# Weight tiles moved by 16 and 32 bytes relative to the moving operands, in a windowed attention, gated FFN and channel MLP kernel

## Chip, cores, metric

One NeuronCore of a Trainium2 chip runs the program. The metric is the time of one execution in microseconds on the device; below, the median of several runs.

## What is computed

Attention over 4 batches, 8 heads, 576 positions and 64 dimensions a head, with a window of 32 (plain for heads 0 to 3, each fourth position for heads 4 to 7); then a gated feed-forward layer with a time shift; then a channel MLP on top of a rank-32 mix over positions:

```python
attn = softmax(where(mask, q @ k.T / 8, -1e9)) @ v          # x: (4, 576, 512)
xk = mu_k * x + (1 - mu_k) * x_prev;  xr = mu_r * x + (1 - mu_r) * x_prev
x = sigmoid(xr @ w_r) * (relu(xk @ w_k) ** 2 @ w_v)         # 512 -> 1024 -> 512
u = x + (x.T @ U @ V).T
out = u + relu(u @ w_ch1) @ w_ch2                           # 512 -> 2048 -> 512
```

## The kernel before

The products run on TensorE as fp32r, each value split into a high and a low part, so that a product takes three matmuls: high weights by high data, low weights by high data, high weights by low data. The low part is what is left after the high part was rounded off (`hi_lo` in the first layers, `part_split` in the last).

The work stands in three blocks in time, read from the timeline.

- **Up to 60 us**: attention of the first batch, loading and converting the weights of the gated layer, and that layer on the first 288 positions in plain fp32 (L1110, L1125).
- **60 to about 340 us**: the gated layer on the other seven pieces of 288 positions. Its three matmuls are L1097, L1098 and L1099, each 128x128 weights by 288 columns. The moving data are the tiles `xk` (in box A's place) and `k2s` (in box B's), 16 pieces of 288 columns each. Between them lie the attention of the later batches (L958, L996, L1014), and the rank-32 mix (L1223 transposes, L1241, L1258).
- **About 340 us to the end**: the channel MLP. It runs in nine visits (`VISITS`) over five groups of positions, each over four or eight of the eight tiles j of 256 hidden channels. Its first product is L1374 to L1376, its second L1462 to L1464, all 128x128 weights by 256 columns. Seven products of sums of blocks stand for the eight of a two-by-two block product; VectorE and ScalarE form the sums.

**Where the tiles lie.** A tile pool gives each tag its place in SBUF once; a tile is made when the first operation on it is recorded, and a new tag goes behind those already there. The weights are pieces of 512 words, 2,048 bytes, in a pool of 42 under the tag `w` (`piece`, names `wh`, `wl`, and `wx` for the plain fp32 ones). In the last block the weights of each fourth tile j (j % 4 == 3) lie in box A and box B instead, into which `take` puts them with `part`; by then `xk` and `k2s` are done. `SHIFT` moves what is in such a box by some words: by 16 words in A, and in B by 16 for units below 10 (weights) and by 64 for those from 10 on (hidden values, which are moving operands). A word is 4 bytes.

`Lazy.__call__` puts a small tile, a pad, ahead of the first tile of the tags in `PADS`: 16 words ahead of `w`, 48 words ahead of `pt`, which lies behind the pool `w`.

By the addresses in the built program all tiles of pool `w` start at 224 (mod 256). The moving tiles (boxes `raw`, `w64`, `x`, `sig`, `xk`, `k2s`, hidden values in B) start at 160; of the pieces of 288 columns (1,152 bytes) the odd ones start at 32. The weights in boxes A and B start at 224. The distance between two addresses is that of the moving operand less that of the weights, modulo 256 bytes.

What orders the work: all operations are recorded, and `plan()` lays them out by a table of ranks (`RANKS`) with its own estimates; each engine then runs its queue in order. Addresses have no part in it.

Of the kernel before, what the change touches and what calls it, by code (L numbers as in the profile page):

```python
# [20 lines left out]
B, H, S, D = 4, 8, 576, 64  # L21
# [182 lines left out]
def tile_attention_mix_channel(  # L204
# [19 lines left out]

    ops = []

    PADS, PADW = ['w', 'pt'], {'w': 16, 'pt': 48}

    class Lazy:

# [388 lines left out]
            a, b = self.c0 + a, self.c0 + (self.n if b is None else b)  # L619
            return [(self.home, u) for u in range(a // Q, (b + Q - 1) // Q)]  # L620

    BOXES = {"A": (1, 4624), "B": (1, 4672), "raw": (4, 1280), "w64": (4, 1024), "x": (2, 2304), "sig": (1, 1152)}
    def SHIFT(tag, unit):
        return 16 if tag == "A" else (16 if unit < 10 else 64) if tag == "B" else 0

    LOOSE = {"pr": 4, "pt": 2, "sig": 1, "d": 2, "m": 1, "y": 1, "rt": 1, "k2": 1, "w32": 3, "raw": 4, "us": 1, "vs": 1}
    boxes = {}
# [2 lines left out]
    def part(tag, i, unit, n):  # L630

        bufs, cols_ = BOXES[tag]
        if (tag, i) not in boxes:
            boxes[tag, i] = Lazy([P, cols_], F32R, tag, f"box{tag}", bufs)
        return Part(boxes[tag, i], unit * Q, n * Q, SHIFT(tag, unit))
# [1168 lines left out]
```

## Time and profile before

| | us |
|---|---|
| runs | 714.62, 715.00, 717.75 |
| median | 715.0 |
| the profiled execution's own time | 713.53 |
| its span (first to last instruction) | 711.8 |
| TensorE busy, of that span | 703.4 |
| VectorE busy | 598.0 |
| ScalarE busy | 421.4 |
| GpSimd busy | 125.9 |

The granted clock of TensorE is 1.0 over the span, the upper of its two levels. The busy time of TensorE doesn't tell its pace, since matmuls overlap in their rows; the time between the starts of two matmuls does. The timeline prints starts to 0.01 us. Finer means come from a stretch of many matmuls: its length, divided by their count.

### The profile page before, as it was taken

How to read it: one execution, taken by the hardware profiler on the slowest of the kernel's cores; microseconds unless marked ns; L12 is line 12 of the kernel's file. 1: busy time of each engine (PE TensorE's matmuls, PEld its weight loads, DVE VectorE, ACT ScalarE, POOL GpSimd, SP SyncE). 2: the span in 40 equal slices, each digit the busy share in tenths (PEclk: the TensorE clock that was granted, in tenths of full speed). 3: DMA queues.
4: the chain of work that ended last, by engine and by line, in shares of the span. 5: the costliest groups of instructions: out<-in, count | busy, mean ns of one | idle time of the engine just before them, and what ended most of it. 6: DMA issues, size and time to landing. Idle time of an engine off the chain costs nothing. (4 is left out here: it accounts for less than half of the span.)

```text
span 711.8 us, 19151 instructions
## 1 busy us (share of the span) xinstructions
PE 703.4 (99%) x7527; PEld 681.2 (96%) x7527; DVE 598.0 (84%) x1528; ACT 421.4 (59%) x1041; POOL 125.9 (18%) x164
## 2 busy tenths in 40 slices
PE   8999999999999999999999999999999999999997
PEld 6788999999999999999899999999999999999997
DVE  5879988788767745889998999999999889898773
ACT  6897886767686846266564554445576445454332
POOL 0001364555463635120000000000000000000000
PEclk9999999999999999999999999999999999999999
DMA  8987258876736631656636556543554210440203
GB/s 319 362 282 236 86 177 279 284 245 211 256 134 227 210 93 46 218 178 210 202 95 194 157 171 210 168 143 90 185 171 134 60 47 18 135 131 31 90 17 118
DMA packets 69979, 117.71 MB, mean 165 GB/s; under 512 B 6144, under 2 KB 41216, under 8 KB 69888
## 3 DMA queue, kind: packets, MB, share of 16 engines
q1 hardware_dynamic: 69888, 116.49, 50.0%
q8 instruction: 59, 0.97, 0.6%
q14 instruction: 32, 0.26, 0.1%
HBM read 85.00 MB, written 31.46 MB: 164 GB/s over the span
## 5 line engine op out<-in xcount | busy, mean ns | idle before, releaser
L1097 PE MATMUL psM<-xk,wh 128*128 128x288 f32 x336 | 100.7, 300 | 0.0
L1098 PE MATMUL psM<-xk,wl 128*128 128x288 f32 x336 | 99.1, 295 | 0.0
L1099 PE MATMUL psM<-xk,wh 128*128 128x288 f32 x336 | 99.1, 295 | 0.0
L1097 PE MATMUL psM<-k2s,wh 128*128 128x288 f32 x224 | 67.0, 299 | 0.0
L1098 PE MATMUL psM<-k2s,wl 128*128 128x288 f32 x224 | 66.1, 295 | 0.0
L1099 PE MATMUL psM<-k2s,wh 128*128 128x288 f32 x224 | 66.0, 295 | 0.0
L1097 PEld LDWEIGHTS psM<-xk,wh 128*128 128x128 f32 x336 | 63.2, 188 | 0.9
L1098 PEld LDWEIGHTS psM<-xk,wl 128*128 128x128 f32 x336 | 63.2, 188 | 0.2
L1099 PEld LDWEIGHTS psM<-xk,wh 128*128 128x128 f32 x336 | 63.2, 188 | 0.0
L1374 PE MATMUL psM<-boxraw,wh 128*128 128x256 f32 x198 | 55.7, 281 | 0.0
L1375 PE MATMUL psM<-boxraw,wl 128*128 128x256 f32 x198 | 55.2, 279 | 0.0
L1376 PE MATMUL psM<-boxraw,wh 128*128 128x256 f32 x198 | 55.2, 279 | 0.0
L1374 PE MATMUL psM<-boxw,wh 128*128 128x256 f32 x186 | 53.1, 285 | 0.7 <-DVE hb L1424 0.5
L1464 PE MATMUL psS<-boxx,wh 128*128 128x256 f32 x192 | 53.5, 279 | 0.0
L495 POOL TENSOR_TENSOR k2s<-k,k2s 128x288 fp32r<-128x288 f32 x49 | 43.2, 884 | 57.7 <-ACT k2s L500 56.0
L1376 PE MATMUL psM<-boxw,wh 128*128 128x256 f32 x186 | 51.9, 279 | 0.0
L1375 PE MATMUL psM<-boxw,wl 128*128 128x256 f32 x186 | 51.9, 279 | 0.0
L791 ACT ACTIVATE pr<-pr,mn 128x64 f32<-128x64 f32 x144 | 48.0, 336 | 5.1 <-DVE mn L782 4.9
L495 POOL TENSOR_TENSOR xk<-m,xk 128x288 fp32r<-128x288 f32 x48 | 41.6, 877 | 31.9 <-ACT xk L500 28.1
L1097 PEld LDWEIGHTS psM<-k2s,wh 128*128 128x128 f32 x224 | 42.1, 188 | 0.4
L1098 PEld LDWEIGHTS psM<-k2s,wl 128*128 128x128 f32 x224 | 42.1, 188 | 0.1
L1099 PEld LDWEIGHTS psM<-k2s,wh 128*128 128x128 f32 x224 | 42.1, 188 | 0.0
(254 smaller groups left out, 2460.2 us busy)
## 6 DMA issues: line engine op xcount, KB each, us to landing
w<-w2raw SPq DMA_DIRECT2D x32, 512.0 KB, 5.1
w<-w1raw SPq DMA_DIRECT2D x20, 512.0 KB, 6.6
w2f<-w SPq DMA_DIRECT2D x32, 256.0 KB, 2.5
ub<-uf SPq DMA_DIRECT2D x32, 256.0 KB, 3.4
ws<-w2f SPq DMA_DIRECT2D x24, 256.0 KB, 3.5
raw<-qk SPq DMA_DIRECT2D x16, 320.0 KB, 6.8
ytmp<-y SPq DMA_DIRECT2D x32, 144.0 KB, 2.0
yb<-ytmp SPq DMA_DIRECT2D x4, 1152.0 KB, 6.2
```

The source lines that it names most:

```text
L495: op("POOL", t, lambda: nc.gpsimd.tensor_tensor(out=out_(), in0=a(), in1=b(), op=ALU.subtract), r, w, 40, lock=True)
L791: nc.scalar.activation(pr[:, d : d + KW], pr[:, d : d + KW], AF.Exp, bias=mn[:, i : i + 1], scale=-1.0, accum_out=sm[:, i : i + 1])
L1097: nc.tensor.matmul(a, lhsT=wh, rhs=xh, start=start, stop=False)
L1098: nc.tensor.matmul(a, lhsT=wl, rhs=xh, start=False, stop=False)
L1099: nc.tensor.matmul(a, lhsT=wh, rhs=xl, start=False, stop=stop)
L1374: nc.tensor.matmul(a, lhsT=wh(*wi), rhs=xh(*ci), start=start and n == 1, stop=False, skip_group_check=True)
L1375: nc.tensor.matmul(a, lhsT=wl(*wi), rhs=xh(*ci), start=False, stop=False, skip_group_check=True)
L1376: nc.tensor.matmul(a, lhsT=wh(*wi), rhs=xl(*ci), start=False, stop=last, skip_group_check=True)
L1464: nc.tensor.matmul(a, lhsT=wh(*wi), rhs=xl(), start=False, stop=stop, skip_group_check=True)
```

## The change

Three numbers that place tiles, one that sizes a box, and one that makes up for the smaller pad:

```diff
-    PADS, PADW = ['w', 'pt'], {'w': 16, 'pt': 48}
+    PADS, PADW = ['w', 'pt'], {'w': 8, 'pt': 56}
...
-    BOXES = {"A": (1, 4624), "B": (1, 4672), "raw": (4, 1280), "w64": (4, 1024), "x": (2, 2304), "sig": (1, 1152)}
+    BOXES = {"A": (1, 4620), "B": (1, 4672), "raw": (4, 1280), "w64": (4, 1024), "x": (2, 2304), "sig": (1, 1152)}
     def SHIFT(tag, unit):
-        return 16 if tag == "A" else (16 if unit < 10 else 64) if tag == "B" else 0
+        return 12 if tag == "A" else (20 if unit < 10 else 64) if tag == "B" else 0
```

The pad ahead of pool `w` shrinks from 64 to 32 bytes, so all its 42 tiles start 32 bytes lower; the pad ahead of `pt` grows by as much, so what lies behind stays. Weights in box A move 16 bytes down, those in box B 16 bytes up. In the built program the starts (mod 256) and the distances are:

| weights in | start before | start after | distance before | distance after |
|---|---|---|---|---|
| pool `w` | 224 | 192 | 192, and 64 for odd pieces of 288 columns | 224, and 96 |
| box A | 224 | 208 | 192 | 208 |
| box B | 224 | 240 | 192 | 176 |

All other tiles start where they started; box A ends 16 bytes earlier. The five engines have the same instructions in the same order in both programs (4,896 rows of TensorE, 1,441 of VectorE, 723 of ScalarE, 95 of GpSimd, 302 of SyncE, with equal neighbours taken together).

## Rows read from the trace of the kernel before

**Rows 1.** The page: span, busy times, and the chain by engine.

```profile
span 711.8 us, 19151 instructions
...
PE 703.4 (99%) x7527; PEld 681.2 (96%) x7527; DVE 598.0 (84%) x1528; ACT 421.4 (59%) x1041; POOL 125.9 (18%) x164
...
PE 47%; DVE 0%; issue 0%
```

**Rows 2.** Windows: busy us (xcount) of PE, PEld, DVE, ACT, POOL; clock, DMA.

```profile
60.00:340.00 280.00, 280.00 (x3670) 273.27 (x3670) 221.15 (x673) 190.69 (x544) 121.32 (x152) 1.00 0.58 192
340.00:400.00 60.00, 57.56 (x463) 54.90 (x462) 56.49 (x122) 31.63 (x62) 0.00 (x0) 1.00 0.55 173
400.00:500.00 100.00, 100.00 (x853) 99.95 (x852) 96.62 (x202) 49.11 (x94) 0.00 (x0) 1.00 0.47 148
500.00:600.00 100.00, 100.00 (x856) 99.64 (x855) 94.18 (x194) 58.62 (x119) 0.00 (x0) 1.00 0.35 106
600.00:700.00 100.00, 100.00 (x879) 99.90 (x878) 82.05 (x161) 41.86 (x82) 0.00 (x0) 1.00 0.29 88
```

**Rows 3.** Groups, stage one: line, tiles, shape, count, busy us, mean ns.

```profile
L1097 PE MATMUL psM<-xk,wh 128*128 128x288 f32 x336 | 100.7, 300 | 0.0
L1097 PE MATMUL psM<-k2s,wh 128*128 128x288 f32 x224 | 67.0, 299 | 0.0
```

**Rows 4.** Timeline, stage one: start us, us, line, tiles, shape, count.

```profile
294.29 0.30 PE L1098 MATMUL psM<-xk,wl 128*128 128x288 f32 x1
294.43 0.29 PE L1099 MATMUL psM<-xk,wh 128*128 128x288 f32 x1
294.56 0.69 PE L1258 MATMUL psS<-vs,g 128*128 128x288 f32 x4
295.08 0.30 PE L1097 MATMUL psM<-xk,wh 128*128 128x288 f32 x1
```

**Rows 5.** Timeline: plain fp32 passes of 288 columns, first block.

```profile
30.29 5.98 PE L1125 MATMUL psM<-xk,wx 128*128 128x288 f32 x24
```

**Rows 6.** Timeline, stage two: matmuls (PE) and weight loads (PEld).

```profile
440.13 0.28 PE L1464 MATMUL psS<-boxx,wh 128*128 128x256 f32 x1
440.14 0.19 PEld L1462 LDWEIGHTS psM<-boxraw,wh 128*128 128x128 f32 x1
440.25 0.28 PE L1462 MATMUL psM<-boxraw,wh 128*128 128x256 f32 x1
```

**Rows 7.** Windows of TensorE: two of stage one, three of stage two.

```profile
133.00:144.00 11.00, 11.00 (x85) 1.00 0.85 306
272.00:283.00 11.00, 11.00 (x86) 1.00 0.21 72
408.00:492.00 84.00, 84.00 (x716) 1.00 0.50 162
...
640.00:666.00 26.00, 26.00 (x232) 1.00 0.11 35
668.00:707.00 39.00, 39.00 (x347) 1.00 0.22 67
```

**Rows 8.** Timeline of TensorE around 407.36 us.

```profile
407.36 0.31 PE L1374 MATMUL psM<-boxraw,wh 128*128 128x256 f32 x1
407.51 0.28 PE L1375 MATMUL psM<-boxraw,wl 128*128 128x256 f32 x1
```

**Rows 9.** Waits of TensorE: us in total, times, longest us.

```profile
PE psM L1374 <- DVE hb L1424: 0.5, 1, 0.5
```

**Rows 10.** Timeline: transposes of 128 columns, stage one.

```profile
70.66 0.71 PE L996 MATMUL psS<-cst_t,pr 128*128 128x128 f32 x5
71.12 0.38 PE L1097 MATMUL psM<-xk,wh 128*128 128x288 f32 x1
```

**Rows 11.** Groups of VectorE: splits of 512-column weights.

```profile
L497 DVE TENSOR_TENSOR wl<-ws,wh 128x512 fp32r<-128x512 f32 x24 | 16.5, 700 | 1.2 <-ACT wh L500 1.2
...
L497 DVE TENSOR_TENSOR wl<-s,wh 128x512 fp32r<-128x512 f32 x12 | 8.2, 684 | 0.1
```

## The prediction

> **What bounds the kernel now.** I read the page first: TensorE is busy for 703.4 of 711.8 us, and half of the chain that ended last is its matmuls [rows 1]. A table by stage shows the same from 60 us on: it has work in every microsecond of the 280 us of the second block (I call 60 to 340 us stage one) and of the 360 us of the channel block (340 to 700, stage two), but for 2.4 us [rows 2]. In stage two its waits for another engine come to 0.5 us [rows 9]. So the end is set by how fast one matmul follows another, and by nothing that the change leaves alone.
>
> That pace isn't the duration of a row. A 288-column matmul is shown with some 300 ns [rows 3] and a 256-column one with 0.28 us [rows 6], but they overlap: in the timeline the next begins 0.13 us after it in stage one [rows 4] and 0.12 us after it in stage two [rows 6]. What to read is the distance between starts, which I call the step. A window also counts what was under way at its start, that is a row's length over one step, 2.2 to 2.4 matmuls. So in stage one 11 us over (85 to 86, less 2.2) is 131 to 133 ns, 132 in the mean; in stage two 84 us over 713.6 is 117.7 ns, and 26 us over 229.6 and 39 us over 344.6 are 113.2 ns [rows 7]. By the start times in the timeline the two steps are 117.8 and 113.3 ns.
>
> **Where addresses can matter.** The weights of the next matmul are loaded while the present one streams its moving operand: the load's row begins within 10 ns of the matmul's [rows 6]. Both read SBUF, and the diff changes only the distance between the two addresses. Full-rate matmuls do lose something there. The plain fp32 passes of the first block stream the same 288 columns at half the rate: 23 steps from 30.29 us to the last start (5.98 less about 0.41 us) are 242 ns each [rows 5], so 121 ns at full rate, and stage one takes 132. Eleven nanoseconds of 132 are a loss of full-rate streaming while weights load; over the 1,680 matmuls of stage one (336 + 224 of each of three lines) that is 18.5 us.
>
> Stage two shows that the loss isn't fixed. With one and the same distance, 192, everywhere, it has two steps, 117.8 and 113.3 ns. Each holds for hundreds of matmuls [rows 7] and flips only where TensorE was held for a moment, as at 407.36 us, where one step is 0.15 us long [rows 8]: by start times it ran at the short step for 2 us ahead of that, and at the long one for 728 matmuls after it, to which the window from 408 us belongs. By start times in the timeline 1,515 of the 3,072 matmuls follow at the long step and 1,483 at the short one; the long stretches of each are those of [rows 7]. So how the two streams lie in time is worth 4.5 ns a matmul. An address moved by 16 or 32 bytes is a shift of one stream against the other, and could do the same.
>
> **Does distance do it?** I took the tiles' addresses from the built program. In before the tiles of the weights lie at 224 (mod 256) and the moving ones at 160, or at 32 for odd pieces of 288 columns. So stage one alternates between distances 192 and 64, and its rows are 0.13 to 0.14 us apart as printed [rows 4]. The four small products of L1258 add two more: the step from 294.43 us is at distance 128, and four steps in 0.52 us from 294.56 us are three at 64 and one at 0 [rows 4]. So 0, 64, 128 and 192 all give 0.13 us: distance does nothing there. But they are all multiples of 64. The new distances (224 and 96 for pool w, 208 for box A, 176 for box B) leave 32, 16 and 48 over a multiple of 64, and no full-rate row of this trace shows one. The one row at 224 is the transposes of L996, which stream 128 columns: five in 0.46 us, the last of them followed by its neighbour after 28 ns, so four steps of 108 ns [rows 10]. They show that a load of 128 weight columns can be that short at such a distance; with half the streaming they don't settle the question.
>
> The Trainium skill has a rule that speaks against any effect: its page "TensorE: Matmul & The Clock Gate", section "Step-by-step: what each phase is for", gives the array two independent read ports into SBUF, one for the moving operand and one for weights. By it the sum is zero in both stages. The equal steps at four distances agree; the two steps at one distance, and the 11 ns that half-rate passes don't pay, don't.
>
> **The change part by part.** No instruction is added, removed or moved: all five engines have the same rows in the same order.
>
> - Pool w by 32 bytes: all 1,680 matmuls of stage one, and three quarters of stage two (three of each four weight tiles j). Cost taken: nothing. The nearest rows are the steps at four distances, 130 ns in four and 0.13 us in each other row. Bounds: one step of the size stage two shows, 1,680 x 4.5 = 7.6 us, either way; farther out, the half-rate floor, 18.5 us down.
> - Boxes A and B by 16 bytes, one up, one down: the last quarter of stage two. With w, this stage has ends at all short steps, 1,515 x 4.5 = 6.8 us less, and all long ones, 1,483 x 4.5 = 6.7 us more. Cost taken: nothing, as the mix stays near half and half. Farther out: 108 ns for all, which needs more than the other engines allow (below).
> - Writes into moved tiles, by VectorE and ScalarE: VectorE splits a 512-column weight in 684 to 700 ns [rows 11], and the kernel has 84 such splits. If each moved by that spread, 16 ns, it is 1.3 us of VectorE, either way, hidden while it has idle time. Taken as nothing.
> - Pad pt grows as w's shrinks, so everything behind stays where it was. No cost.
>
> What is next late if stage two gets faster: VectorE. From 400 to 500 us it works 96.6 of 100 us, from 500 to 600 us 94.2 [rows 2]. All short steps would take 3.5 us from the first of these (787 of its steps are long), and VectorE has 3.4 to give. From 340 to 600 us it has 3.5 + 3.4 + 5.8 = 12.7 us in all, and after 600 us another 5 us would go at 108 ns: so stage two can't gain more than some 17 us, and what it can gain in the first of these hundreds is 3.4. Losses have no such end. In stage one VectorE works 221 of 280 us [rows 2], and gains up to 18 us fit.
>
> **Sum.** Zero against the profiled execution's own 713.5 us (span 711.8 and 1.7 around). The median of the runs is 1.5 higher: 715.0.
>
> **Rivals.**
> 1. Faster, by the short step: the new distance makes the short step the one that is fallen into. Stage two alone: 715.0 - 6.8 = 708.2. If stage one falls by a like 4.5 ns, 715.0 - 14.4 = 700.6. For it: the short step exists, and the only row at 224 is lean. Against: stage one doesn't react to four other distances, and from 400 to 500 us VectorE leaves hardly room for it.
> 2. Slower, by the long step: the new distances, and the jumps of 16 bytes between w and the boxes inside one stretch, push TensorE out of the short step, in which it now runs nearly all of 600 to 707 us [rows 7]. 715.0 + 6.7 = 721.7; with stage one a like step up, 729.3. It decides once some 800 of the 1,483 short steps are lost (800 x 4.5 = 3.6 us). For it: the short step lasted longest where nothing disturbed it. Against: nothing but equal steps at four distances.
> 3. The change doesn't do what it says. By the addresses of the built program it does: tiles of pool w at 192 (mod 256), weights in box A at 208, in box B at 240, moving operands unmoved at 160 and 32. I give it no chance of its own.
>
> **How the numbers follow.** A measurement here tells about 0.5%, 3.6 us, from no change. Forecast (no distance effect, the mix within its spread; its own range 711.5 to 718.5, as the runs before span 714.6 to 717.8): 0.38. Rival 1: 0.34, of which 0.22 is stage two alone and 0.12 with stage one. Rival 2: 0.28, of which 0.19 is stage two alone. The range runs from rival 1 with stage one to rival 2 without it, 701 to 722; beyond it I leave some 0.07 below and 0.12 above.
>
> **What would show it.** Step in stage one: 132 ns in windows without other work means no effect of w's 32 bytes; under 130 or over 134 means that there is one. Stage two: matmuls in a window of 100 us, 853, 856 and 879 now [rows 2]; all short would be 886, all long 851. By tile: the steps while a weight of box A or B loads against those while one of w does. VectorE's busy share in 400 to 500 us near 100 with waits of TensorE for it means that a gain was cut there. I'd be wrong if stage one moved at all, since four distances say that it doesn't, or if a third step appeared in stage two.

## The result and the profile after

The changed kernel takes **721.5 us** in the median (721.0 to 723.3), the kernel before 716.3 in the same comparison: a ratio of 1.0079, interval 1.0055 to 1.0103. It is slower by 0.8%. The predicted 715.0 was no change; the time lies inside the range, and on the side to which 0.28 was given.

The page of the profile after, with the span, the busy times and the chain by engine, as [rows 1]:

```profile
span 719.8 us, 19151 instructions
...
PE 712.2 (99%) x7527; PEld 690.3 (96%) x7527; DVE 600.2 (83%) x1528; ACT 421.7 (59%) x1041; POOL 125.8 (17%) x164
...
PE 47%; DVE 0%; issue 0%
```

The same bound, the same 7,527 matmuls, and 8.8 us more of TensorE's busy time; VectorE and ScalarE have theirs as before. The profiled executions stand 8.0 us apart, the medians 5.2: the one shown of before (713.5 us with its 1.7 around the span) was a good draw, 2.8 us under the median of this comparison. In after there is little to draw, its runs lie within 2.3 us. Why, the experiments show.

Where the time is, the windows by stage tell (busy us and count of PE, PEld, DVE, ACT, POOL; clock, DMA share, GB/s, as [rows 2]):

```profile
60.00:340.00 280.00, 279.61 (x3653) 272.81 (x3647) 220.44 (x672) 190.09 (x543) 121.02 (x152) 1.00 0.58 191
340.00:400.00 60.00, 58.49 (x453) 56.05 (x452) 55.86 (x120) 31.28 (x61) 0.00 (x0) 0.97 0.55 174
400.00:500.00 100.00, 100.00 (x844) 99.85 (x843) 95.88 (x201) 48.75 (x93) 0.00 (x0) 1.00 0.47 148
500.00:600.00 100.00, 100.00 (x844) 99.92 (x843) 93.46 (x191) 57.85 (x116) 0.00 (x0) 1.00 0.35 106
600.00:700.00 100.00, 100.00 (x845) 99.98 (x844) 81.23 (x159) 40.55 (x78) 0.00 (x0) 1.00 0.24 75
```

In stage two 100 us now hold 844, 844 and 845 matmuls, 853, 856 and 879 before. The prediction reckoned 851 for a stage at nothing but long steps: after is under that, so there must be a step longer than the long one. The clock has a small part in it. It is granted in full from 400 us on; the 0.97 before that is one fall to the lower level, 1.2 GHz (0.52 granted from 348 to 350 us), behind two holds. The five matmuls of 512 columns that stand there took 1.41 us before and 2.48 us now (timeline of TensorE, before and after):

```profile
348.54 1.41 PE L1710 MATMUL psS<-zero 128*128 128x512 f32 x5
348.54 2.48 PE L1710 MATMUL psS<-zero 128*128 128x512 f32 x5
```

By the start times, matmul for matmul, after is 0.1 us behind before at 347 us, 1.0 at 353 us and 8.0 at the end: the fall accounts for about 1 us of the eight, and seven are lost behind it, at the full clock. The kernel with the boxes alone, below, has 0.89 and 0.94 of the clock in 340 to 360 us and is faster all the same; the one with all weights at 224 has a mean clock of 1.000 and is slow.

Nor is a wait the cause. The only wait of a line of the channel MLP for VectorE is that of [rows 9], and shorter (us in total, times, longest):

```profile
PE psM L1374 <- DVE hb L1424: 0.3, 1, 0.3
```

The same stretches as in [rows 7], TensorE alone:

```profile
133.00:144.00 11.00, 11.00 (x85) 1.00 0.80 293
272.00:283.00 11.00, 11.00 (x86) 1.00 0.21 72
408.00:492.00 84.00, 84.00 (x710) 1.00 0.49 157
640.00:666.00 26.00, 26.00 (x222) 1.00 0.18 54
668.00:707.00 39.00, 39.00 (x331) 1.00 0.26 78
```

Read as the prediction read them, less 2.4 matmuls that were under way: 84 us over 707.6 is 118.7 ns, 26 over 219.6 is 118.4, 39 over 328.6 is 118.7. All three stretches have nearly one mean step, where before had 117.8 and 113.3. The two stretches of stage one count 85 and 86 matmuls, as before.

By the start times of the timeline, stage two begins at 338.06 us (337.96 before), and from its first matmul of L1374 to its last one it takes 377.7 us (369.8): 7.9 of the span's 8.0 us. Its steps under 140 ns are 3,040 with a mean of 118.45 ns, in before 3,030 with 115.66: 2.79 x 3,036 is 8.5 us more, and ten more of them 1.2 us; the longer steps, in which TensorE was held, are 18 with 4.1 us against 28 with 6.3. That gives 7.5 of the 7.9 us. The rest stands in the pairs with another matmul between, where the fall of the clock lies.

### The profile page after: what moved, and what is told of

Its sections match the earlier page's. It is cut to its first block, busy times and chain, and to the rows that moved or that the text cites. A ratio compares the mean times of both kernels' runs of the same rounds, so it can differ in the third digit from the quotient of the medians.

```text
span 719.8 us, 19151 instructions
## 1 busy us (share of the span) xinstructions
PE 712.2 (99%) x7527; PEld 690.3 (96%) x7527; DVE 600.2 (83%) x1528; ACT 421.7 (59%) x1041; POOL 125.8 (17%) x164
## 2 busy tenths in 40 slices
DMA packets 69979, 117.71 MB, mean 164 GB/s; under 512 B 6144, under 2 KB 41216, under 8 KB 69888
## 5 line engine op out<-in xcount | busy, mean ns | idle before, releaser
L1097 PE MATMUL psM<-xk,wh 128*128 128x288 f32 x336 | 101.3, 301 | 0.0
L1099 PE MATMUL psM<-xk,wh 128*128 128x288 f32 x336 | 99.5, 296 | 0.0
L1098 PE MATMUL psM<-xk,wl 128*128 128x288 f32 x336 | 98.1, 292 | 0.0
L1097 PE MATMUL psM<-k2s,wh 128*128 128x288 f32 x224 | 67.5, 301 | 0.0
L1099 PE MATMUL psM<-k2s,wh 128*128 128x288 f32 x224 | 66.3, 296 | 0.0
L1098 PE MATMUL psM<-k2s,wl 128*128 128x288 f32 x224 | 65.5, 292 | 0.0
L1098 PEld LDWEIGHTS psM<-xk,wl 128*128 128x128 f32 x336 | 63.9, 190 | 0.3
L1097 PEld LDWEIGHTS psM<-xk,wh 128*128 128x128 f32 x336 | 63.2, 188 | 0.9
L1099 PEld LDWEIGHTS psM<-xk,wh 128*128 128x128 f32 x336 | 63.1, 188 | 0.0
L1374 PE MATMUL psM<-boxraw,wh 128*128 128x256 f32 x198 | 55.8, 282 | 0.0
L1374 PE MATMUL psM<-boxw,wh 128*128 128x256 f32 x186 | 53.1, 285 | 0.3 <-DVE hb L1424 0.3
L1098 PEld LDWEIGHTS psM<-k2s,wl 128*128 128x128 f32 x224 | 42.6, 190 | 0.1
L1097 PEld LDWEIGHTS psM<-k2s,wh 128*128 128x128 f32 x224 | 42.1, 188 | 0.4
L1099 PEld LDWEIGHTS psM<-k2s,wh 128*128 128x128 f32 x224 | 42.0, 188 | 0.0
```

What stands on the lines that cost most here:

```text
L1097: nc.tensor.matmul(a, lhsT=wh, rhs=xh, start=start, stop=False)
L1098: nc.tensor.matmul(a, lhsT=wl, rhs=xh, start=False, stop=False)
L1099: nc.tensor.matmul(a, lhsT=wh, rhs=xl, start=False, stop=stop)
L1374: nc.tensor.matmul(a, lhsT=wh(*wi), rhs=xh(*ci), start=start and n == 1, stop=False, skip_group_check=True)
```

## Experiments

Two theories stood at the start. **Theory A**: the distance itself sets the step, and only multiples of 64 have the short one. **Theory B**, one of the two causes that rival 2 of the prediction names: each distance would do, but the jumps of 16 bytes between pool w and the boxes push TensorE out of the short step. All kernels below but the first and the fifth are edits of the kernel before.

### One distance at a time

A kernel of nothing but full-rate matmuls, in blocks of 60 in the order wh, wl, wh with two pieces of moving operand in turn; between blocks TensorE is held. Its core:

```python
for n, d, blocks in TESTS:            # columns, distance, blocks
    for b in range(blocks):
        w0 = 8 + (256 - d) // 4       # weights' start, in 4-byte elements
        for t in range(20):
            wh = w0 + t % 4 * 128 + t // 4 % 3 * 2048
            wl = wh + 1024
            xh, xl = 8 + t % 2 * 512, 2056 + t % 2 * 512
            for w, x in ((wh, xh), (wl, xh), (wh, xl)):
                nc.tensor.matmul(acc[:, :n], lhsT=W[:, w:w+128], rhs=X[:, x:x+n], ...)
        ...                           # the block's bank is copied out
```

> This kernel leaves out the whole computation and writes zeros: it is 98 blocks of 60 fp32r matmuls in the kernel's order (high weights, low weights, high weights), each block held until its bank is copied out, at one distance between moving operand and next weights: every multiple of 16 bytes from 0 to 240, with 256 columns (4 blocks each) and 288 columns (2 blocks each), and 184 and 188 with 256 columns. Theory A (the residue over 64 bytes decides): at 0, 64, 128 and 192 blocks of 256 columns run at 113.3 or at 117.8 ns a step, at the other twelve distances none runs at 113.3 and the mean is 118 to 119; with 288 columns all stand at 132 within 2 ns. Theory B (jumps of the distance inside a stretch decide, not the distance): with the distance held fixed through a block, blocks at 113.3 ns appear at 208, 224 and 176 as at 192. If the two read ports never met, all blocks of 256 columns would have one step.

The timeline of this kernel, TensorE (start us, length us, line, tiles, shape, count, idle ahead): one block each at distance 64, 208 and 224, the four at 192, and the two blocks of 288 columns at 64:

```profile
138.89 7.33 PE L43 MATMUL acc<-X,W 128*128 128x256 f32 x60 [0.52 <-DVE gone L45]
...
391.54 7.08 PE L43 MATMUL acc<-X,W 128*128 128x256 f32 x60 [0.52 <-DVE gone L45]
399.14 7.33 PE L43 MATMUL acc<-X,W 128*128 128x256 f32 x60 [0.52 <-DVE gone L45]
406.99 7.09 PE L43 MATMUL acc<-X,W 128*128 128x256 f32 x60 [0.52 <-DVE gone L45]
414.60 7.08 PE L43 MATMUL acc<-X,W 128*128 128x256 f32 x60 [0.52 <-DVE gone L45]
422.20 7.34 PE L43 MATMUL acc<-X,W 128*128 128x256 f32 x60 [0.52 <-DVE gone L45]
...
453.60 7.36 PE L43 MATMUL acc<-X,W 128*128 128x256 f32 x60 [0.52 <-DVE gone L45]
...
586.73 8.17 PE L43 MATMUL acc<-X,W 128*128 128x288 f32 x60 [0.55 <-DVE gone L45]
595.45 8.20 PE L43 MATMUL acc<-X,W 128*128 128x288 f32 x60 [0.55 <-DVE gone L45]
```

A block is 59 steps and some 0.4 us of the last row, so 7.08 us is the short step and 7.33 the long one. At distance 192 four like blocks, one after the other, took both: the two steps of stage two, in a kernel that has no other work. Mean steps of the blocks, from the start times behind the first ones of a block (the first block at distance 0 ran in part at the lower clock, 213 ns a step, and is left out):

| distance | 256 columns, ns | 288 columns, ns |
|---|---|---|
| 192 | **113.3**, 117.8, **113.3**, **113.3** | 133.3 |
| 64 | 117.8 | 131.8, 132.3 |
| 0, 128 | 120.0, 118.7 | 131.7, 133.4 |
| 32, 48, 112 | 116.6 to 117.8, 116.7, 116.7 (one 120.0) | 130.0 to 133.4 |
| 208, 176, 224 | 117.8, 118.7, 118.4 | 131.1 and 133.3 at 208 and 224 |
| the other multiples of 16 | 117.4 to 120.1 | 130.0 to 133.4 |

Of sixteen distances only 192 showed 113.3 here, and of the change's new distances none; 184 and 188, tried besides, took 118.3 to 118.5. Theory A as it was put falls, though: 0, 64 and 128 are multiples of 64 and have no short step in this kernel. Theory B fares no better: it expected blocks at 113.3 at 208, 224 and 176, since a block keeps one distance. At 288 columns each distance takes 130 to 133 ns, and the four that stage one showed 131.7 to 133.4. So the evidence of stage one, four distances with equal steps, was true to the 0.01 us to which those rows are printed, and says nothing of 256 columns.

### Pool w alone, the boxes alone, and all at 224

Three edits share one comparison, in which the kernel before has a median of 715.6 us. The quotients of the medians are 1.0055, 0.9970 and 1.0060; each lies inside the interval of the ratio given below.

Pool w alone:

```diff
-    PADS, PADW = ['w', 'pt'], {'w': 16, 'pt': 48}
+    PADS, PADW = ['w', 'pt'], {'w': 8, 'pt': 56}
```

> Pool w alone moves by 32 bytes (distances 224 and 96), boxes A and B stay at 192. Theory A: three quarters of stage two at 118.3 ns, the box quarter still at 113.3 or 117.8; stage one 132.3; time 720 to 721.5. Theory B: the distance still jumps between 224 and 192, so all of stage two is near 118.3: 721.5. Before in the same comparison: 715 to 717.

719.6 us, ratio 1.0068 (1.0045 to 1.0090). Windows of TensorE (us, busy us and count; clock, DMA):

```profile
400.00:500.00 100.00, 99.99 (x849) 1.00 0.46 148
500.00:600.00 100.00, 100.00 (x848) 1.00 0.34 106
600.00:700.00 100.00, 100.00 (x851) 1.00 0.25 77
```

The steps at 224 are 2,274 with a mean of 118.27 ns; the box weights, still at 192, have 116.09. Against 115.66 for all of before's that is 2,274 x 2.61 = 5.9 us and 0.3 more, and the span is 6.0 us longer, at a mean clock of 1.000. Pool w is nearly the whole loss.

The boxes alone:

```diff
-    BOXES = {"A": (1, 4624), ...}
+    BOXES = {"A": (1, 4620), ...}
...
-        return 16 if tag == "A" else (16 if unit < 10 else 64) if tag == "B" else 0
+        return 12 if tag == "A" else (20 if unit < 10 else 64) if tag == "B" else 0
```

> Boxes A and B alone move by 16 bytes (208 and 176), pool w stays at 192. Theory A: the box quarter (768 matmuls) at 118.2, the other three quarters at 113.3 or 117.8 as they fall: 715 to 718.5. Theory B: three distances in one stretch, so the short step is lost everywhere: 720 to 722. Stage one 132.3 by both.

713.5 us, ratio 0.9968 (0.9947 to 0.9988): **faster**, and under what either theory expected. Windows of TensorE:

```profile
400.00:500.00 100.00, 100.00 (x863) 1.00 0.46 148
500.00:600.00 100.00, 100.00 (x864) 1.00 0.34 106
600.00:700.00 100.00, 100.00 (x868) 1.00 0.29 89
```

That is ten and eight more than before in the first two [rows 2] and eleven fewer in the third, where the profiled execution of before ran almost wholly at the short step; the spans of the two profiled executions, 711.4 and 711.8, hardly differ, since before's was a good draw. The box steps themselves are long, 118.56 ns at 176 and 117.94 at 208, but the 2,267 steps at 192 between them have 114.73: with jumps at every change of box, the short step isn't lost.

All weights at 224, so there is no jump between w and boxes:

```diff
-    PADS, PADW = ['w', 'pt'], {'w': 16, 'pt': 48}
+    PADS, PADW = ['w', 'pt'], {'w': 8, 'pt': 56}
...
-    BOXES = {"A": (1, 4624), ...}
+    BOXES = {"A": (1, 4616), ...}
...
-        return 16 if tag == "A" else (16 if unit < 10 else 64) if tag == "B" else 0
+        return 8 if tag == "A" else (8 if unit < 10 else 64) if tag == "B" else 0
```

> All weights at one new distance: pool w, box A and box B at 224 (96 for odd pieces in stage one), no jumps. Theory A: no step of 113.3 anywhere in stage two, mean 118.3: 721.5. Theory B: one fixed distance, so two steps hold as before and the time comes back to 713 to 718.

719.9 us, ratio 1.0078 (1.0054 to 1.0102). Windows of TensorE:

```profile
400.00:500.00 100.00, 100.00 (x846) 1.00 0.46 148
500.00:600.00 100.00, 100.00 (x845) 1.00 0.34 106
600.00:700.00 100.00, 100.00 (x847) 1.00 0.24 76
```

Without any jump the stage is as slow as after: 3,042 steps with a mean of 118.31 ns, and no stretch of twelve steps with a mean under 117.5. With the boxes' result this ends theory B. The distance 224 has no short step, and three quarters of stage two were put on it.

### What follows a stretch at another distance

Why do the boxes alone gain? This kernel takes, for each distance, ten times 12 matmuls at it and then 24 at 192, with no hold between; after that blocks at 192 with the moving operand at eight starts (mod 256), and ten held blocks of 36.

```python
for d in range(0, 256, 16):
    block([p for _ in range(10) for p in ((256, d, 4, 8), (256, 192, 8, 8))])  # columns, distance, triples, start
for at in range(0, 64, 8):
    for _ in range(3):
        block([(256, 192, 20, at)])
for _ in range(10):
    block([(256, 192, 12, 8)])
```

> This kernel leaves out the whole computation and writes zeros. First, for each of the 16 distances d that are multiples of 16 bytes, one run without a hold: ten times 12 matmuls at d and 24 at 192, 256 columns. Then held blocks of 60 at 192 with the moving operand starting at each multiple of 32 bytes (mod 256), three each, and ten held blocks of 36 at 192. Theory C (at 192 there are two ways to run, and each coming back to it chooses anew): the stretches at 192 end at 113.3 or 117.8 ns a step and at nothing else; which of them depends on the d that went before, more often 113.3. Theory A as it stood (any distance that is a multiple of 64 has the short step) would have 0, 64 and 128 at 113.3 in the first part as well. If only the distance counts and not the address, the blocks with other moving starts run at 113.3 or 117.8 too.

Timeline of TensorE, columns as in the first kernel: the groups of 360 matmuls at 32, 64, 80, 192, 208 and 224 (ten times 12 at the distance and 24 at 192), and two of the held blocks:

```profile
97.09 41.48 PE L38 MATMUL acc<-X,W 128*128 128x256 f32 x360 [0.52 <-DVE gone L45]
...
181.09 41.14 PE L38 MATMUL acc<-X,W 128*128 128x256 f32 x360 [0.52 <-DVE gone L45]
222.74 42.67 PE L38 MATMUL acc<-X,W 128*128 128x256 f32 x360 [0.52 <-DVE gone L45]
...
521.43 42.66 PE L38 MATMUL acc<-X,W 128*128 128x256 f32 x360 [0.52 <-DVE gone L45]
564.61 41.60 PE L38 MATMUL acc<-X,W 128*128 128x256 f32 x360 [0.52 <-DVE gone L45]
606.73 42.73 PE L38 MATMUL acc<-X,W 128*128 128x256 f32 x360 [0.52 <-DVE gone L45]
...
875.87 4.37 PE L38 MATMUL acc<-X,W 128*128 128x256 f32 x36 [0.51 <-DVE gone L45]
880.76 4.50 PE L38 MATMUL acc<-X,W 128*128 128x256 f32 x36 [0.52 <-DVE gone L45]
```

The group at 192 throughout held the long step for all 360 matmuls and did not leave it by itself. By the start times the stretches at 192 end at 113.3 or 117.8 and at nothing else. After 16, 32, 48, 64, 112, 144, 160, 176 and 208 the short step came each time; after 80, 96 and 224 the long one each time (0, 128 and 240 differ between the first time and the nine others). The ten times are one repeating pattern and not ten draws: where a short stretch follows a short one, the stretch between may have set the step or only kept it. Three groups show that a stretch at another distance **can change** the step: behind 128 and 240 it went from long to short, behind 0 from short to long (the first stretches of that group ran in part at the lower clock). That 208 and 176 set the short step, or 224 the long one, isn't shown by this; the kernels below show how often 208 and 176 do. At 64 the steps had 113.3 from the second time on, the short step that the first kernel had not met there. The blocks with eight starts ran at 113.3 or 117.8, so both steps don't hang on the start that the other blocks share. Of the ten held blocks six were short and four long.

### Each box alone

```diff
-    BOXES = {"A": (1, 4624), ...}
+    BOXES = {"A": (1, 4620), ...}
...
-        return 16 if tag == "A" else (16 if unit < 10 else 64) if tag == "B" else 0
+        return 12 if tag == "A" else (16 if unit < 10 else 64) if tag == "B" else 0
```

> Box A alone moves by 16 bytes (208), pool w and box B stay at 192. Theory C: 512 matmuls near 118 ns, the 2,560 at 192 chosen anew at each return, after 208 less often at the short step than after 176 (as seen where both boxes had moved): 713 to 717. Theory B (jumps push TensorE out of the short step) has all of it at the long one: 721.

Box A alone: 713.2 us, ratio 0.9967 (0.9946 to 0.9987). Windows of TensorE:

```profile
400.00:500.00 100.00, 99.88 (x861) 1.00 0.47 148
500.00:600.00 100.00, 100.00 (x866) 1.00 0.35 106
600.00:700.00 100.00, 100.00 (x873) 1.00 0.29 88
```

The kernel before has 716.1 in this comparison. 2,508 steps at 192 have a mean of 114.33 ns, 499 at 208 have 117.71.

```diff
-        return 16 if tag == "A" else (16 if unit < 10 else 64) if tag == "B" else 0
+        return 16 if tag == "A" else (20 if unit < 10 else 64) if tag == "B" else 0
```

> Box B alone moves by 16 bytes (176), pool w and box A stay at 192. Theory C: 256 matmuls near 118.5 ns, 2,816 at 192 chosen anew at each return, mostly short after 176: 711 to 714. Theory B: 721.

Box B alone: 714.1 us, ratio 0.9972 (0.9956 to 0.9987); 2,761 steps at 192 with 114.98 ns, 255 at 176 with 118.49. Each box alone gains what both together gain. To see how, I followed the stretches of eight and more matmuls at 192 in the start times of one execution each: what was the step ahead of a break, and what after it? (A few between the two steps count as not short; where the border is set moves some counts by one to three.)

| kernel | break | short step kept | long step turned short |
|---|---|---|---|
| before | holds | 8 of 15 | 5 of 7 |
| box A alone | 208 | 37 of 39 | 5 of 13 |
| box B alone | 176 | 34 of 35 | 4 of 6 |
| both boxes | 208, 176 | 53 of 54 | 5 of 18 |

In before only holds decide, and a hold loses the short step about as often as it finds it. A stretch of box weights at 208 or 176 all but never loses it and now and then finds it; in 23 of 37 cases it leaves the long step as it was, so it does not set the step, as the repeating pattern above may suggest. What it finds outweighs the box steps' own price, some 3 ns for each of 250 to 760 steps.

Inside a stretch nothing changes. If each step over 122 ns counts as a hold too, then none of the stretches of twelve and more steps at 192 in these four executions (26 in before with 2,885 steps; 56, 56 and 64 in the others) goes from one step to the other between its ends. The step changes at a hold or a break and nowhere else, which speaks for the breaks as the cause of the gain and against the writes into the boxes, the rival named ahead of the next version.

### Five versions meant to gain more

If the box steps are the price and the return is the gain, fewer box steps might do better. First, only units 10 and 11 of box B at 176:

```diff
-        return 16 if tag == "A" else (16 if unit < 10 else 64) if tag == "B" else 0
+        return 16 if tag == "A" else (16 if unit < 10 else 60 if unit < 12 else 64) if tag == "B" else 0
```

> As before, but of the moving operands in box B two of eight pieces (hidden values of even tiles j) start 16 bytes lower, so 176 matmuls of stage two are at 176 and all others at 192. Theory C: these cost at most 176 x 5 = 0.9 us and make TensorE choose anew in every second visit of a tile j; after 176 it took the short step each time in the chain of blocks without a hold, so the matmuls at 192 should average 113.5 to 114.5 in place of 115.6: 709 to 713 against some 716 of before. If instead what made a_only and b_only faster was something else about the boxes (their writes), nothing changes: 715 to 717.

714.9 us, ratio 0.9990 (0.9975 to 1.0004): no gain is shown, a miss, and what the rival in the same text, the boxes' writes, had forecast. The execution profiled is the slowest of twelve, 716.8 us. In it the short step was kept in 14 of 20 returns, and the long one turned in 6 of 22; the steps at 192 have 116.30 ns. Breaks at the same distance of 176 act otherwise at this place than in box B's lower units; what differs wasn't settled.

Second, units 0 and 1 of box A at 208:

```diff
-        return 16 if tag == "A" else (16 if unit < 10 else 64) if tag == "B" else 0
+        return (12 if unit < 2 else 16) if tag == "A" else (16 if unit < 10 else 64) if tag == "B" else 0
```

> As before, but of the weights in box A only the first piece (80 matmuls) starts 16 bytes lower, at 208. Theory C: cost under 0.4 us, and a new choice wherever that piece is used, which is for each fourth tile j: matmuls at 192 average 114 to 115, time 711 to 714.

713.95 us, ratio 0.9977 (0.9963 to 0.9991). A gain, not above that of the whole box; 78 steps at 208, and 115.27 ns at 192, more than the 114 to 115 expected.

Third, both:

```diff
-        return 16 if tag == "A" else (16 if unit < 10 else 64) if tag == "B" else 0
+        return (12 if unit < 2 else 16) if tag == "A" else (16 if unit < 10 else 60 if unit < 12 else 64) if tag == "B" else 0
```

> Both of these: 256 matmuls at 176 or 208. Theory C: the most frequent new choices at a cost of 1.3 us at most, matmuls at 192 near 113.5 to 114.2, time 708.5 to 712.

714.3 us, ratio 0.9990 (0.9977 to 1.0002): a miss as well, no gain is shown. The mean at 192 is 115.58 ns.

Last, box A at 208 and box B at one of the two distances that did best in the second of the kernels with matmuls alone, 64 and 48. First 64:

```diff
-    BOXES = {"A": (1, 4624), ...}
+    BOXES = {"A": (1, 4620), ...}
...
-        return 16 if tag == "A" else (16 if unit < 10 else 64) if tag == "B" else 0
+        return 12 if tag == "A" else (48 if unit < 10 else 64) if tag == "B" else 0
```

> Pool w stays at 192, box A goes to 208 (16 bytes), box B to 64. In the chain without holds 64 ran at 113.8 ns itself and was followed by the short step each time. Theory C with stretches of 9 or more matmuls needed to leave a step: matmuls at 208 near 117.8, at 64 near 113.8 to 115, at 192 near 114.3: 711.5 to 714, that is 1 us under the kernel with box A alone moved. If 64 falls to the long step as in its held blocks: 714 to 716.

713.05 us, ratio 0.9981 (0.9966 to 0.9997): inside what was expected, and not shown to be better than box A alone (0.9967). The nine matmuls named there no run tests. Box B's 255 steps at 64 have 115.12 ns against 118.56 at 176, so the kernel does have a short step there; 2,260 steps at 192 have 114.64.

Then 48:

```diff
-        return 12 if tag == "A" else (48 if unit < 10 else 64) if tag == "B" else 0
+        return 12 if tag == "A" else (52 if unit < 10 else 64) if tag == "B" else 0
```

(The line taken out is that of the version just above.)

> Pool w stays at 192, box A goes to 208, box B to 48, which in both sweeps ran at 116.7 ns and was followed by the short step each time. Theory C: matmuls at 208 near 117.8, at 48 near 116.7, at 192 near 114.3 or less: 712 to 714. Theory A's last remnant (any other distance just costs its own step, and what runs at 192 is untouched) would have 716 to 717.

714.2 us, ratio 1.0001 (0.9986 to 1.0017): no gain, though a stretch at 48 had been followed by the short step each time in the kernel of matmuls alone. Here, after a stretch at 48, the short step was kept in 8 of 18 cases only, against 20 of 20 after 64 in the version before it.

Box A alone, box B alone and both boxes so beat the kernel before by 0.3%, and the changed one by 1.1% as worked out from two comparisons (0.9967 over 1.0079). Of the five that followed, two beat the kernel before by 0.2%, and none does better than these three.

## Why the prediction was wrong

**What bounds the kernel** was right: TensorE's step and nothing else. VectorE is no part of the story, at 95.9 of 100 us in the first hundred of stage two.

**The step that failed** is the cost of pool w in stage two, "Cost taken: nothing. The nearest rows are the steps at four distances". These rows, [rows 4], are of 288 columns, and printed to 10 ns, coarser than the 4.5 ns in question. At 288 the matmuls alone show no distance that stands out either, 130.0 to 133.4 ns over all sixteen; at 256 columns they span 113.3 to 120.1. The indifference of one shape was carried to another. The prediction held the right row, two steps at one distance in stage two [rows 7], and read it as a draw that every distance would make; at 224 no run shows a short step: pool w alone at 224 has 118.27 ns, all weights there 118.31, the blocks of matmuls alone 118.4. **The term mis-sized** is "the mix stays near half and half": taken as 0, it measured 2.79 ns x 3,036 = 8.5 us in the profiled executions, against a loss of 5.2 us in the medians, since before's profiled execution was a good draw.

**Rival 2 came out, in half of its cause.** Its 721.7 lies 0.2 from the measured 721.5. It named two causes, the new distances and the jumps between w and the boxes. The new distance of pool w does take the short step away. The jumps aren't needed: all at 224 is as slow without them, and the boxes' jumps alone make the kernel faster. That the number fits so well is luck. The 6.7 us were put on the median of 715.0, while the loss was 8.0 us in the profiled executions and 5.2 in the medians; and the bound, "all long ones", isn't one, since the step at 224 isn't the long step but a mixture of 115 to 123 ns with a mean of 118.3. The prediction named a third step in stage two as a sign that it was wrong, and it is there.

**Stage one** was right: 132.26 ns before and 132.32 after over 1,600 steps each. Underneath it did react. From L1097 to L1098 the step grew from 131.6 to 134.4 ns, from L1098 to L1099 it shrank from 132.5 to 129.8. In the timeline after it is 0.13, 0.14 and 0.13 us (start us, length us), as [rows 4]:

```profile
294.56 0.30 PE L1097 MATMUL psM<-xk,wh 128*128 128x288 f32 x1
294.69 0.30 PE L1098 MATMUL psM<-xk,wl 128*128 128x288 f32 x1
294.83 0.30 PE L1099 MATMUL psM<-xk,wh 128*128 128x288 f32 x1
294.96 0.30 PE L1097 MATMUL psM<-xk,wh 128*128 128x288 f32 x1
```

So the row-by-row test of the prediction, a mean step moved or not, was too coarse to tell "no effect" from "effects that cancel". The floor of 121 ns for 288 columns, taken from the plain fp32 passes, no run came near: the lowest step of the matmuls alone is 130 ns.

**Boxes A and B.** The price of their own steps, 2 to 3 ns on some 760, was missed, and so was the gain on the steps at 192 around them. In the changed kernel only the price is left: with w at 224 there is no 192 to come back to. Its box steps have 118.6 ns against the 116.09 of the kernel with pool w alone moved, 762 x 2.5 = 1.9 us, and so far apart are the medians, 721.5 and 719.6 (of two comparisons). This fits the parts, which don't add: pool w alone is +0.7%, the boxes alone -0.3%, and both together +0.8%, not +0.4%, each within some 0.2%.

**Writes into moved tiles** at nothing: right. VectorE's splits of [rows 11] moved from 700 and 684 to 702 and 687 ns, and its total by 2.2 us beside idle time.

The Trainium skill's rule that the prediction weighed (page "TensorE: Matmul & The Clock Gate", section "Step-by-step: what each phase is for") gives the streaming operand and the weights separate read ports. The runs decide against reading it as "addresses don't matter": with nothing but the distance changed, the same matmuls took 113.3 ns in three blocks of four at 192 and 118.4 in all four at 224. By the Trainium skill's page "SBUF — State Buffer", section "SBUF: two separate sides", TensorE's reads wait for no other engine. The kernel of matmuls alone agrees in so far as both steps stand there with no other engine at work inside a block; what within TensorE makes them isn't shown.

**What stays open.** Why 192 and 64 show a short step and the others don't; what in a hold or a break decides which step follows; why breaks at 176 keep the short step in one part of box B and less often in another; why a stretch at 48 was followed by the short step in the kernel of matmuls alone and often not in the full one. The runs show that it is so, and not by which part of the chip.

## What to carry to other kernels

Where a kernel's end is set by back-to-back matmuls whose weights change each time, the place of the weights relative to the moving operand is worth up to 6% of a step (113.3 to 120.1 ns at 256 columns): measure it in the very shape, with blocks at one distance each, and don't carry an equal pace over from another width. Where the trace shows two paces in one stage, ask which addresses allow the faster one before reckoning with the average. Move one group of tiles at a time: here one move hid the gain of another.

## What the runs showed that was not expected

- One distance, one instruction stream, two steps: at 192 the blocks of 60 took 113.3 or 117.8 ns, changed in the stretches followed here only at a hold or a stretch at another distance, and stayed at 117.8 through 360 matmuls without one.
- A stretch of 12 matmuls at another distance can change what follows: behind 128 and 240 the step at 192 went from long to short. In the full kernel stretches at 208 and 176 kept the short step in 124 of 128 cases and turned the long one short in 14 of 37.
- Distance is felt at 16 bytes: 113.3 (or 117.8) at 192, 117.8 at 208, 118.7 at 176, 118.4 at 224, and up to 120.1 at 16, 96 and 144.
- The runs of before over all comparisons lie between 711.8 and 718.9 us, those of after, which has no short step, between 721.0 and 723.3. The two-step draw may be most of before's spread; with one trace of before that isn't shown. The clock is little of it: 36 of its 85 runs beside the experiments have a mean clock of 1.000, and they lie between 711.8 and 717.6, 0.6 us lower in the mean than the other 49.
